# The front of an adaLN / S4 convolution / SwiGLU kernel in a new order: logs and right-hand sides first, two steps' tables, then u

## The chip, the cores and the metric

The kernel runs on one core of a Trainium2 chip. Times are device microseconds of that core, median of several runs. The engines of the core are TensorE (PE in the profile, its weight loads PEld), VectorE (DVE), ScalarE (ACT), GpSimd (POOL) and the queues that issue transfers, above all that of SyncE (SP). Each engine takes its own instructions in order and waits on semaphores for the others.

## The reference

For an input of 2048 rows and 640 columns, the reference computes

```
mod = silu(c) @ w_mod                      # six vectors of 640: sa, ca, ga, sb, cb, gb
h   = layernorm(x) * (1 + ca) + sa
K   = Re( sum_n C * exp(dt*A*l) * dt*B )   # one filter of 2048 taps per column, 128 states each
x   = x + ga * ( causal_conv(h, K) + h * Dskip )     # in the reference by FFT of length 4096
h   = layernorm(x) * (1 + cb) + sb
x   = x + gb * ( (silu(h @ w1) * (h @ w3)) @ w2 )    # inner width 1728
```

All of it is float32. The parameters A, B, C are complex numbers of 640 x 128.

## The kernel before, in words

The kernel has a first part, the convolution with everything that prepares it, and a second part, the feed-forward with its weights split in two for fast float32 matmuls. The change lies in the first some 160 us of the first part, called the front here; what follows is untouched.

**The filter.** A tap number is split as l = 64 a + b. For 16 channels (one step; there are 40) the kernel makes tables of the magnitudes and the phases of 128 states at 64 + 32 points, and a product on TensorE over the 128 states gives all taps of a channel. A step's work is a fixed series, each with a short name in the code: PH makes integer phases on POOL (two products, `phases`, L473 and L474); AB, CO and SI turn them into cosines and sines on ACT; PA, XA, PQ, XQ make exponents by matmuls against small right-hand sides r2, r1 and `sel` and an Exp on ACT (`exps` does a pair of steps); E1, E2, A1, A2 multiply magnitude by cosine and sine on DVE (L498, L501, L505, L509); `kg` is the product on TensorE; K, pt and uk scale it and make its first transform stage.

**The parameters.** `polar` (L239) turns A, B, C and dt into log magnitudes (`la`, `lm`, transposed on TensorE for the exponents) and integer phases (`thi`, `phi`). It is a generator in parts: the factors up to their squares; logarithm and angle; then the rows for `la` and `lm` and the last steps of the phase. It is done for the first 128 channels ahead of everything, and for the other 512 in the first four turns of the loop below. Its working space is the third of the `uk` buffers (`flat[2]`), the same room that later takes pieces of w_mod.

**The modulation.** `mod_sums` (L300) sums a piece of silu(c) @ w_mod: five matmuls, one for each block of 128 rows of K, the first four in the four groups of 32 columns of the array, the fifth again in the first group. A second matmul against the column `one4` adds the four groups. Eight such pieces (`mod_early`) give sa, ca and ga in the front, in the PSUM banks pb and pk in turn; five larger ones (`mod_cols`) come at the end of the front and give the feed-forward's vectors. `mod_shift` (L319) makes the row sa / (1 + ca), broadcasts it into PSUM by ten recorded matmuls (`pr`), copies it (`rrow`), and by a multiply (`rc`), twelve recorded matmuls (`ps`) and a copy makes `shift`, the row scaled by the transform of a constant.

**u.** `ln1_norm` normalizes two tiles of x, `u_stage1` (L395) makes the first transform stage of one tile in PSUM banks Z and A or B, adds the shift on the way out and stores u to DRAM. There are 16 tiles; `u_load` brings u back by frequency.

**Order.** A scheduler places each engine's instructions by their place in the program and by modelled readiness; ACT's instructions (`act`, `acopy`, `act_set`) keep the order of the program in all of the front. After the opening lines, a loop of ten turns (`tk`, L777) does the steps' tables, two u tiles a turn, the second pass of the parameters, and at its end the five `mod_cols`. Their w_mod pieces go through two rooms of `flat[2]`. When the last is done the pool `pre` closes, and the space goes to the convolution's second stage (`stage2`, L571). From there to 365 us rounds of four steps repeat one written order of words.

The opening, whose order is the subject, is this (L730 to 771, shortened):

```
first = polar(d0, V); next(first); next(first)
for j in range(4): ln1_load(j)
... r2; rest of first; do("PH", 0); r1
... five mod_early, loads
mod_shift(); act_set("natural_log_exp_and_others")
exps(0); ln1_norm(0); exps(2); ln1_norm(1)
do("PH", 1); do("PH", 2); AB, CO, SI of step 0
u_stage1(0); u_stage1(1); ln1_norm(2); AB, CO, SI of step 1
... three mod_early; mod_gate(); u_stage1(2); u_stage1(3)
```

## Time and profile before

| | us |
|---|---|
| median of three runs | 971.03 |
| the three runs | 970.67, 971.03, 975.4 |
| the profiled execution | 975.08 |
| its span, first to last instruction | 973.3 |
| PE busy in the span | 896.1 (92%) |
| DVE busy | 714.1 (73%) |
| ACT busy | 543.0 (56%) |
| POOL busy | 282.4 (29%) |

Rows of the profile give the engine, the line of the code (L102 is line 102), the operation, output and inputs with their shapes, how often it occurs, and its times. A row in the order of time begins with its start and its length in us; what stands in brackets is the idle time of the engine before it and what ended that. A line with x10 is several instructions of one kind merged, with the time from the first start to the last end. A row of the chain has only start, length and the instruction or the transfer. A row of a group has the busy time of all and the mean in ns. A float32 matmul of the code is recorded as two instructions. The clock is TensorE's granted clock as a share of full speed.

### The profile page before, as it was taken

Reading aid. Unit: us, or ns where it says so; the run is one execution under the profiler, and the core shown is the slowest. Engines: PE = TensorE matmul, PEld = TensorE weight load, DVE = VectorE, ACT = ScalarE, POOL = GpSimd, SP = SyncE. Lnnn points to the kernel's source line nnn. Section 1 sums busy time; section 2 is a strip of 40 time slices with the busy share of each in tenths; the row PEclk is TensorE's granted clock in tenths of the full one; section 3 lists DMA queues with packets and bytes.
Section 4 is the critical chain, followed back from the end, with each engine's and each line's share of the span. In section 5 each row is a group of like instructions: output and inputs, shape, how many; then the busy total and the mean of one; then the engine's idle time right before and its main releaser. Section 6 shows DMA issues by size and latency. Waiting matters only on the chain.

```text
span 973.3 us, 20145 instructions
## 1 busy us (share of the span) xinstructions
PE 896.1 (92%) x7984; PEld 675.4 (69%) x7984; DVE 714.1 (73%) x1259; ACT 543.0 (56%) x795; POOL 282.4 (29%) x278
## 2 busy tenths in 40 slices
PE   4978787889888899899999999999999999999998
PEld 2534444666666666567888888777888888888886
DVE  5598865999999996767666665677786766654675
ACT  4568675999999984236433333455743333333332
POOL 1372343455455641113422220121252222200000
PEclk8555777999999999899999999999999999999999
DMA  9463576655665688785213112895422221113443
GB/s 267 143 228 131 198 202 179 163 147 140 170 162 145 171 224 245 220 216 194 91 55 108 55 55 78 234 272 187 146 84 64 77 66 53 54 41 94 149 150 122
DMA packets 103571, 140.73 MB, mean 145 GB/s; under 512 B 20564, under 2 KB 62676, under 8 KB 103476
## 3 DMA queue, kind: packets, MB, share of 16 engines
q1 hardware_dynamic: 99668, 129.34, 46.0%
q0 software_dynamic: 2304, 7.74, 2.4%
q10 hardware_dynamic: 1504, 2.36, 0.8%
q8 instruction: 63, 1.03, 0.4%
q14 instruction: 32, 0.26, 0.1%
HBM read 107.94 MB, written 31.46 MB: 143 GB/s over the span
## 4 chain that ended last, share of the span: by engine, by line
PE 76%; ACT 9%; DVE 7%; DMA 4%; issue 3%; POOL 0%; ACTq 0%; SPq 0%; DVEq 0%; POOLq 0%
PE ps L102 55%; PE p L571 6%; ACT A L135 3%; PE pz L613 3%; PE pk L522 2%; PE pt L540 2%; ACT cs L135 2%; DMA zs<-zt 2%; PE pq L445 2%; PE pa L435 1%; PE pm L305 1%; PE pu L412 1%; ACT uk L138 1%; DMA uk<-in_w_mod_dram 1%; PE pm L316 1%
## 5 line engine op out<-in xcount | busy, mean ns | idle before, releaser
L102 DVE TENSOR_TENSOR s<-ps,s 128x512 f32<-128x512 f32 x138 | 94.9, 688 | 80.4 <-PE ps L102 79.5
L473 POOL TENSOR_TENSOR ph<-thi,iota 128x1024 int32<-128x1024 int32 x40 | 91.9, 2298 | 154.4 <-DVE A L505 54.0
L102 DVE TENSOR_TENSOR gl<-rw,gh 128x640 fp32r<-128x640 f32 x87 | 78.2, 899 | 65.2 <-ACT gh L102 65.1
L102 ACT CAST gh<-rw 128x640 fp32r<-128x640 f32 x87 | 63.3, 727 | 104.2 <-PE ps L102 63.4
L571 PE MATMUL p<-uk,s 128*64 128x256 f32 x640 | 79.4, 390 | 14.0 <-ACT uk L138 5.8
L102 PE MATMUL ps<-xA,gh 128*128 128x512 f32 x280 | 87.8, 392 | 0.4 <-ACT xA L102 0.4
L102 PE MATMUL ps<-gh,uh 128*128 128x512 f32 x224 | 87.5, 391 | 0.0
L102 PE MATMUL ps<-gl,uh 128*128 128x512 f32 x224 | 87.2, 389 | 0.0
L102 POOL TENSOR_TENSOR S<-rw 128x256 f32<-128x256 f32 x46 | 36.8, 801 | 170.7 <-DVE S0l L102 160.0
L102 PE MATMUL ps<-gh,ul 128*128 128x512 f32 x208 | 81.1, 390 | 0.0
L571 PEld LDWEIGHTS p<-uk,s 128*64 128x64 f32 x640 | 45.9, 139 | 37.8 <-issue 9.7
L498 DVE TENSOR_TENSOR E<-A,cs 128x1024 f32<-128x1024 f32 x40 | 60.4, 1511 | 3.2 <-ACT cs L135 2.5
L102 PEld LDWEIGHTS ps<-xA,gh 128*128 128x128 f32 x280 | 52.1, 188 | 13.0 <-ACT xA L102 0.9
L102 PE MATMUL ps<-xA,gl 128*128 128x512 f32 x140 | 54.6, 390 | 0.0
L474 POOL TENSOR_TENSOR ph<-ph,phi 128x512 int32<-128x512 int32 x40 | 48.5, 1213 | 5.0 <-DVE phi L297 2.0
L540 PE MATMUL pt<-s,K 128*64 128x128 f32 x640 | 48.3, 291 | 1.4 <-ACT uk L138 1.4
L505 DVE TENSOR_TENSOR A<-A,ph 128x1024 f32<-128x1024 f32 x40 | 48.9, 1223 | 0.0
L102 ACT ACTIVATE s<-ps 128x512 f32<-128x512 f32 (+1 forms) x33 | 19.7, 597 | 51.3 <-PE ps L102 51.3
L102 PEld LDWEIGHTS ps<-gl,uh 128*128 128x128 f32 x224 | 42.0, 188 | 9.0
L102 PEld LDWEIGHTS ps<-gh,uh 128*128 128x128 f32 x224 | 42.0, 188 | 8.7
L522 PE MATMUL pk<-E 128*32 128x64 f32 x1280 | 45.9, 233 | 1.5 <-issue 0.9
L613 PE MATMUL pz<-Y,i 64*128 64x128 f32 x640 | 44.4, 282 | 2.8 <-issue 2.7
(255 smaller groups left out, 2270.4 us busy)
## 6 DMA issues: line engine op xcount, KB each, us to landing
rw<-in_w_dram SPq DMA_DIRECT2D x52, 320.0 KB
us<-u SPq DMA_DIRECT2D x16, 640.0 KB
s<-in_s_dram SPq DMA_DIRECT2D x40, 256.0 KB
i<-in_i_dram SPq DMA_DIRECT2D x40, 256.0 KB
rw<-in_wg_dram SPq DMA_DIRECT2D x31, 320.0 KB
rw<-in_wu_dram SPq DMA_DIRECT2D x28, 320.0 KB
uk<-us SPq DMA_DIRECT2D x32, 256.0 KB
zs<-zt SPq DMA_DIRECT2D x32, 256.0 KB
```

The source lines that it names most:

```text
L102: ins = fn(*args, **kw)
L135: return tc.keep_in_program_order(S.activation(*args, **kw))
L138: return tc.keep_in_program_order(S.copy(out, in_))
L445: keep(PE.matmul(pQ[s][:, rr, :256], w[r, t, :], bc(sel[r, js], 2, NA) if i else r1[r, js, :], start=(i == 0), stop=(i == 1), tile_positio ...
L473: hold(G.tensor_tensor(p, bc(thi[:, sl], 2, NPH), bc(iota, 1, SD), op=OP.mult))
L474: keep(G.tensor_tensor(p[:, :, :NA], p[:, :, :NA], bc(phi[:, sl], 2, NA), op=OP.add))
L498: keep(V.tensor_tensor(EC[s][:, :, 1:3, :], AA[s][:, :, 1:3, :], mid(cs[s]), op=OP.mult))
L505: keep(V.tensor_tensor(A[:, :, 1:3, :], A[:, :, 1:3, :], mid(ph[s]), op=OP.mult))
L522: keep(PE.matmul(pk[dq * 32:dq * 32 + 32, g, :], x[:, g * 4 + dq, 1, :], x[:, g * 4 + dq, 0:3:2, :], start=(st == 0), stop=(st == 1), tile ...
L540: keep(PE.matmul(pt[c * 64:c * 64 + 64, g, :], kk[:, g, :], s1[:, c, :], start=True, stop=True, tile_position=(0, c * 64)))
L571: keep(PE.matmul(p2[par * 64:par * 64 + 64, pi, c, :], s2[:, pi * 2 + par, c * 64:c * 64 + 64], uk[:, 0:kn + 1:kn, f, :], start=True, stop ...
L613: ins = keep(PE.matmul(pz[:, par, (g % 2) * 2 + pi, :], i1[r, pi, c, :], Y[r, pi, c, :], start=(c == 0), stop=(c == 1), tile_position=(par ...
```

## The change

The constants `selx` and `stepx` get a small array of their own, `selstep`, which is the first transfer on SP's queue; `misc` has a new column c1c instead. r2, made from them, is the first DVE instruction after the initial memsets. `polar` becomes a class with the same instructions in parts that can be ordered: for the first 128 channels the order is now factors, log, rows, angle, phase, and the rows of `la` and `lm` have a split space each. The second pass keeps its places in the loop. In the sums the fifth block is divided into four quarters of the columns, one for each group. The broadcast of the row takes 128 columns of weights in place of 64, and `shift` is read from it by two scaled copies on ACT; `rc` and `ps` are gone. In the opening, PH, AB, CO and SI of steps 0 and 1 and the first pair of exponents come before the modulation sums; the tables of step 0 follow LN1's first two tiles; the product of step 0 and the tables of step 1 follow the first two u tiles. Of the three late sums, the second is in bank Z in place of pk.

```diff
-    misc = np.concatenate([selx, stepx, s1r, c1, one4, toq, tog], axis=1)
+    misc = np.concatenate([s1r, c1, np.tile(c1[0], 2)[:, None], one4, toq, tog], axis=1)
+    selstep = np.concatenate([selx, stepx], axis=1)
...
+    l2f = [t3[:, DC + 2 * DC * i:DC + 2 * DC * (i + 1)] for i in range(2)]
...
+    nc.sync.dma_start(selstep, a["selstep"])
     nc.sync.dma_start(cT, a["c"])
...
-    def polar(cs, E):
...
+    class Polar:
...
+        def rows(self):
...
             for i, dst in enumerate((la, lm)):
...
-            both = l2[:, :2 * nk * P].rearrange("n (b s c) -> n b s c", s=2, c=32)
+                both = self.l2[i].rearrange("n (b s c) -> n b s c", s=2, c=32)
...
     def mod_sums(w, pm):
 
         n = w.shape[2]
-        for k in range(KD):
-            g = slice(k % 4 * NA, k % 4 * NA + NA)
-            PE.matmul(pm[g, :n], scb[:, k], w[:, k, :], start=(k < 4), stop=(k > 0), tile_position=(0, g.start))
+        last = [slice(g * n // 4, (g + 1) * n // 4) for g in range(4)]
+        for g in range(4):
+            r = slice(g * NA, g * NA + NA)
+            PE.matmul(pm[r, :n], scb[:, g], w[:, g, :], start=True, stop=False, tile_position=(0, r.start))
+        for g, c in enumerate(last):
+            r = slice(g * NA, g * NA + NA)
+            PE.matmul(pm[r, c], scb[:, 4], w[:, 4, c], start=False, stop=True, tile_position=(0, r.start))
...
         for k in range(KD):
-            PE.matmul(pr[:64, k * P:(k + 1) * P], r[:, k:k + 1].broadcast_to([P, 64]), ident, start=True, stop=True)
+            PE.matmul(pr[:, k * P:(k + 1) * P], r[:, k:k + 1].broadcast_to([P, P]), ident, start=True, stop=True)
+        for hh in range(2):
+            h = slice(hh * 64, hh * 64 + 64)
+            act(shift[h], pr[h, hh * 320:hh * 320 + 320], AF.Copy, scale=c1c[h])
         V.tensor_copy(rrow[:64], pr[:64, :D])
-        rc = pm_.tile([P, WC], F32, name="part", bufs=2)[:, :KD * 2 * NA].rearrange("p (k c) -> p k c", k=KD)
-        V.tensor_tensor(rc, bc(c1, 1, KD), bc(r, 2, 2 * NA), op=OP.mult)
...
-        V.tensor_copy(shift, ps[:, :320])
...
+    V.tensor_tensor(r2, bc(selx, 2, NB), bc(stepx[:, :NB], 1, NA), op=OP.mult)
     act_set("natural_log_exp_and_others")
...
-    first = polar(d0, V)
-    next(first)
-    next(first)
+    first = Polar(d0, V, l2f)
+    first.factors()
+    first.log()
+    first.rows()
+    first.angle()
+    first.phase()
+    V.tensor_tensor(r1, bc(selx, 2, NA), bc(stepx[:, NB:], 1, NA), op=OP.mult)
     for j in range(4):
         ln1_load(j)
-    V.tensor_tensor(r2, bc(selx, 2, NB), bc(stepx[:, :NB], 1, NA), op=OP.mult)
-    for _ in first:
-        pass
     do("PH", 0)
-    V.tensor_tensor(r1, bc(selx, 2, NA), bc(stepx[:, NB:], 1, NA), op=OP.mult)
+    do("PH", 1)
+    for n in ("AB", "CO", "SI"):
+        do(n, 0)
+    for n in ("AB", "CO", "SI"):
+        do(n, 1)
+    act_set("natural_log_exp_and_others")
+    exps(0)
     for i, t in enumerate(("pb", "pk", "pb", "pk", "pb")):
         mod_early(i, wm[i], t)
...
     mod_shift()
-    act_set("natural_log_exp_and_others")
-    exps(0)
     ln1_norm(0)
+    for n in ("E1", "E2", "A1", "A2"):
+        do(n, 0)
     exps(2)
-    ln1_norm(1)
-    do("PH", 1)
-    do("PH", 2)
-    for n in ("AB", "CO", "SI"):
-        do(n, 0)
     u_stage1(0)
     u_stage1(1)
+    ln1_norm(1)
+    do("kg", 0)
+    for n in ("E1", "E2", "A1", "A2"):
+        do(n, 1)
+    do("PH", 2)
     ln1_norm(2)
-    for n in ("AB", "CO", "SI"):
-        do(n, 1)
-    for i, t in enumerate(("pb", "pk", "pb")):
+    for i, t in enumerate(("pb", "Z", "pb")):
         mod_early(5 + i, wg[i], t)
     mod_gate()
     u_stage1(2)
     u_stage1(3)
-    rest = polar(d1, G)
+    rest = Polar(d1, G, [l2, l2])
...
             if tk == 2:
-                next(rest)
+                rest.log()
+                rest.angle()
...
         if tk == 0:
-            next(rest)
+            rest.factors()
         if tk == 3:
-            next(rest, None)
+            rest.rows()
+            rest.phase()
```

127 lines of the change are left out of this document (64 added, 63 removed).

## The prediction

> **What bounds the kernel now.** I read the page first, then the stretches, then the chain of waits, then the order of time in the front. The profiled execution took 975.08 us, 1.78 us more than its span. It is the upper of the three runs (970.67, 971.03, 975.4), 4.05 us above their median; differences found in the trace are therefore taken off its own 975.08 and then off the median 971.03.
>
> ```profile
> span 973.3 us, 20145 instructions
> ...
> PEclk8555777999999999899999999999999999999999
> ```
>
> The clock line says that TensorE is granted about half speed from the second slice (24 us) to the fourth and about 0.7 to the seventh. Next, the stretches (length, then busy us of PE, PEld, DVE, ACT, POOL, then the granted clock, DMA share and GB/s):
>
> ```profile
> 0.00:10.00 10.00, 0.48 (x8) 0.31 (x9) 4.62 (x19) 3.24 (x7) 0.20 (x4) 1.00 0.86 227
> 10.00:20.00 10.00, 6.56 (x33) 3.18 (x25) 8.37 (x24) 4.75 (x10) 2.98 (x2) 0.80 1.09 341
> 20.00:30.00 10.00, 10.00 (x53) 5.74 (x52) 2.71 (x10) 2.71 (x4) 0.00 (x0) 0.50 0.97 290
> 30.00:40.00 10.00, 7.57 (x38) 5.56 (x36) 6.59 (x20) 4.74 (x6) 5.19 (x7) 0.50 0.39 142
> 40.00:50.00 10.00, 9.28 (x76) 3.90 (x74) 5.95 (x11) 7.12 (x8) 5.54 (x5) 0.66 0.07 30
> 50.00:110.00 60.00, 51.82 (x564) 28.22 (x564) 54.29 (x102) 42.94 (x53) 26.44 (x29) 0.54 0.48 177
> 110.00:164.00 54.00, 39.75 (x574) 21.85 (x576) 39.32 (x64) 34.98 (x40) 21.52 (x14) 0.83 0.74 209
> ```
>
> DVE is full from 50 to 110 us (54.29 of 60) but idle for 21.76 of the first 50 us. PE at half clock is nearly full beside it (51.82 of 60). The front therefore has two engines at their limit after 50 us and much idle DVE before. Where the front ends, the chain shows:
>
> ```profile
> 139.26 9.70 DMA uk<-in_w_mod_dram
> ...
> 149.09 2.69 PE pm L305 x10
> ...
> 163.52 3.23 PE p L571 x16
> ```
>
> The first product of the convolution's second stage (L571) starts at 163.5 us, behind the last five column sums and the w_mod transfers that feed them. These transfers are issued only when the second parameter pass has left its room, which the next two rows show: the phase is written at 110.34 and the queue issues at 110.84.
>
> ```profile
> 110.34 0.42 DVE L297 TENSOR_SCALAR phi<-uk 128x512 int32<-128x512 f32 x1
> ...
> 110.84 2.31 SPq L206 DMA_DIRECT2D uk<-in_w_mod_dram  x3
> ```
>
> So whatever brings the 110.3 us point forward brings the front's end forward, as long as the 53 us behind it keep their length. The rounds that follow repeat one written order, with no dependence on when they began; I carry a gain of the front unchanged to the end.
>
> **The change, part by part.** First the parameter pass of the first channels.
>
> ```profile
> 8.43 2.29 DVE L737 TENSOR_TENSOR r<-misc 128x2048 fp32r<-128x2048 f32 x1
> ...
> 10.63 0.29 DVE L257 SCALAR_TENSOR_TENSOR uk<-uk 128x128 f32<-128x128 f32 x1
> ...
> 13.75 1.94 POOL L473 TENSOR_TENSOR ph<-thi,iota 128x1024 int32<-128x1024 int32 x1 [13.30 <-DVE thi L274]
> 13.85 1.99 DVE L288 TENSOR_TENSOR uk<-lt,uk 128x128 f32<-128x128 f32 x1
> ...
> 16.51 0.37 ACT L138 CAST la<-pT 128x256 fp32r<-128x256 f32 x1 [2.84 <-PE pT L291]
> ...
> 17.12 0.29 DVE L288 TENSOR_TENSOR uk<-lt,uk 128x128 f32<-128x128 f32 x1
> ...
> 18.39 0.37 ACT L138 CAST lm<-pT 128x256 fp32r<-128x256 f32 x1 [1.30 <-PE pT L291]
> ```
>
> The table r2 (2.29 us) goes ahead of everything. Its operand selstep is 64 KB and one more issue on SP's queue ahead of c and the parameters; by the row at 110.84 an issue lasts at most 2.31 / 3 = 0.77 us, so the parameters land up to 0.8 us later; I take half of that. r2 then fills DVE time that is idle while the parameters travel, and L257, which now waits until 10.63 behind r2, no longer does; I take half a microsecond gained there. Rows before angle means that la and lm wait for no arctangent: five DVE steps and a table load go out of their way, so lm, now 18.39, comes at about 13.5. The two halves l2f remove the wait of the second cast on the first transposes; that is inside this. Angle and phase then come later in that pass, covered by the transposes and the first exponents' matmuls.
>
> At one place a price must be weighed. L288 took 1.99 us beside POOL's product and 0.29 without it, so one meeting costs 1.7 us. The new order brings a second phase product into this pass. I take one meeting as now, and 1.7 us more as the upper end. The Trainium skill, page "SBUF — State Buffer", section "Who interferes with whom", states that a DVE instruction with two SBUF inputs and a GpSimd instruction that reads SBUF lock each other out for a whole instruction; the trace agrees (1.99 against 0.29 us). By that rule both products would block, and the sum would come 1.7 us higher.
>
> Second, the sums and the shift of LN1.
>
> ```profile
> 31.51 0.16 DVE L317 COPY cols<-pm 128x2 f32<-128x2 f32 x1 [1.19 <-PE pm L316]
> ...
> 34.62 2.40 PE L330 MATMUL pr<-ident,cols 128*64 128x128 f32 x10 [2.43 <-DVE cols L326]
> ...
> 36.81 1.76 PE L339 MATMUL ps<-ident,part 128*64 128x128 f32 x12
> ...
> 39.08 0.47 DVE L341 COPY shift<-ps 128x320 f32<-128x320 f32 x1
> ...
> 43.59 3.46 PE L305 MATMUL pm<-uk,scb 128*32 128x256 f32 x20
> ...
> 158.55 1.91 PE L305 MATMUL pm<-uk,scb 128*32 128x384 f32 x10 [1.99 <-DMA uk<-in_w_mod_dram]
> ```
>
> At half clock two sums of 256 columns take 3.46 us, 1.73 each. The code's five matmuls are ten in the row, two passes each; by their tile positions four K blocks can run side by side and the fifth follows alone, so a pass is 1.73 / 4 = 0.43; the fifth in quarters takes a quarter of it, 0.11. A sum becomes 1.73 - 2 x 0.32 = 1.08, 0.65 less. Five such sums, then two of 256 and one of 128 columns: 7.5 x 0.65 = 4.9 us of PE. It could also be nothing, if three more weight loads per pass (8 in place of 5) are what sets the pace; they are hidden behind matmuls in the row. The removed matmuls ps give 1.76 us of PE, their copy 0.47 of DVE, and the multiply for rc on the same 128x320 shape I price at the same 0.47. The broadcast keeps ten matmuls of 128 columns (2.40), with wider weights. Two scaled copies of 64x320 go to ACT instead; ACT's 128x256 cast above is 0.37, so 0.8 to 1.0 us there, before LN1's first tiles.
>
> Third, the order. With no exponents' matmuls among them, the five sums' chain should end some 6 us before 31.5. Two table steps move from behind the first u tiles to before them.
>
> ```profile
> L498 DVE TENSOR_TENSOR E<-A,cs 128x1024 f32<-128x1024 f32 x12 | 16.3, 1359 | 1.4 <-ACT cs L135 0.7 <-PE pk L522 0.7
> ...
> L505 DVE TENSOR_TENSOR A<-A,ph 128x1024 f32<-128x1024 f32 x11 | 13.6, 1237 | 0.0
> ...
> L501 DVE TENSOR_TENSOR E<-A,cs 128x512 f32<-128x512 f32 x11 | 10.3, 935 | 0.0
> L509 DVE SCALAR_TENSOR_TENSOR A<-ph,A 128x512 f32<-128x512 f32 x11 | 8.0, 727 | 0.0
> ```
>
> A step's tables take 1.36 + 1.24 + 0.94 + 0.73 = 4.26 us, two of them 8.5 us, taken out of the full stretch and put where DVE is idle. On ACT, the sines of two steps and their one table load come before the first exponents:
>
> ```profile
> 20.07 1.02 ACT L135 ACTIVATE A<-pa 128x1024 f32<-128x1024 f32 x1
> ...
> 30.15 0.60 ACT L135 ACTIVATE A<-pq 128x512 f32<-128x512 f32 x1 [2.92 <-PE pq L445]
> ...
> 43.43 1.04 ACT L135 ACTIVATE cs<-ph 128x1024 f32<-128x1024 int32 x1
> 44.49 1.28 ACT L135 ACT_TABLE_LOAD   x1
> 45.79 1.15 ACT L135 ACTIVATE cs<-cs,hp 128x1024 f32<-128x1024 f32 x1
> ...
> 47.79 0.67 ACT L138 COPY u<-pu 128x640 f32<-128x640 f32 x1
> ```
>
> A step's sines take 1.04 + 1.15 + 1.04 (the sine as the absolute value) = 3.23 us, a pair of exponent steps 2 x (1.02 + 0.60) = 3.24, a load 1.28. With the first phases at about 17.5, ACT does 6.5 of sines, 1.3 of load and 3.2 of exponents and ends them at 28.5, now 30.75. Shift, LN1 of two tiles and the second exponents follow; the first u copy, now 47.79, comes at about 36. Behind these waiting ACT steps are queued the shift and LN1, and PE's u matmuls wait for both.
>
> The moved steps pass other queues too. POOL makes the second step's phases ahead of LN1's small steps: its 2.98 and 0.00 us busy from 10 to 30 leave room, no cost. SP's loads keep their order behind selstep; the u stores come earlier, into the stretch with a DMA share of 0.07. The first kernel product keeps its PSUM bank until the gate, so one late sum takes bank Z between two u tiles: sum, copy and columns, about 2.5 us in which the next u tile's first half waits; PE has the other late sums and the product itself meanwhile, so I count nothing, and 2.5 us if that cover is gone.
>
> The sum goes by DVE. Up to 110 us it is busy 4.62 + 8.37 + 2.71 + 6.59 + 5.95 + 54.29 = 82.53 us, less 0.94 for rc and the shift's copy: 81.6. Its idle time up to there is now 27.5. In the new order I estimate 3.5 before the parameters (5.4 less r2, plus the issue), 2 in the rest of the pass, 4 while ACT does sines and exponents (copies of the sums, r1 and the statistics of LN1 remain to fill it; 20 to 40 us had 10.7 idle), 2 up to 50 us (now 4.05), and 6 in the loop (now 5.7): 17.5. The phase would be written at 81.6 + 17.5 = 99.1, or 11.2 us before 110.34.
>
> PE as the check: it is busy 85.7 us up to 110, and 85.7 - 4.9 - 1.8 = 79.0 from 9.5 on could end at 88.5 with no idle at all; 99.1 leaves 10.6 idle where it has about 15 now. That is tight at half clock, so I take 2 us off: 9.2. In the 53 us behind, the last sum (1.91 on the chain) loses three eighths, 0.7; the one before it is followed by a transfer and counts nothing. In all 9.9, say 10 us. From 975.08 that is 965.1; from the median, 961.0.
>
> **The rivals.** First, TensorE is the bound. At half clock PE and DVE wait for each other, and what moves on DVE leaves PE's own work where it is. If the front follows PE with today's idle time, only the five early sums' 5 x 0.65 = 3.3 us remain of the gain: 968. For it: 51.82 of 60 busy. Against it: the same PE line has idle time in 30 to 40 us that the tables now fill. That the moved work changes nothing at the end because transfers set 163.5 anyway falls in with this; against that stands the issue at 110.84, half a microsecond behind the phase.
>
> Second, slower. PE takes its queue in order. If the first steps' pq matmuls stand ahead of the modulation sums, they wait for ACT, whose sines now precede the exponents, and the sums wait behind them. Four sums and their columns (1.1 + 1.0 each) would begin when the first exponents are out, at about 27 to 30, and end near 38 in place of 31.7; shift and LN1's first u follow 6 us later than now. It decides once the first u copy on ACT comes after 47.79; with the 6 us carried through the u tiles, the time is 977.
>
> Third, TensorE goes to full clock in the denser front.
>
> ```profile
> 62.81 1.34 PE L404 MATMUL pu<-rrow,misc 1*64 1x320 f32 x8 [1.52 <-DVE u L417]
> ...
> 108.48 0.77 PE L404 MATMUL pu<-rrow,misc 1*64 1x320 f32 x8
> ```
>
> The same eight matmuls took 1.34 us at half and 0.77 at full clock. PE's 51.82 would then be near 30 and DVE alone the bound; its 5.7 us of idle time in that stretch would go too: 956. Against it: PE was busy 10.00 of 10.00 in 20 to 30 us and the clock stayed 0.50. The Trainium skill, "TensorE: Matmul & The Clock Gate", Part 1, says about 3.4 us of sustained activity releases the clock; the trace does not agree in that stretch.
>
> **How the numbers follow.** A measurement here tells about 0.5%, 4.9 us, from no change (the three runs span 4.7). Forecast 0.56, full clock 0.11, TensorE bound 0.16, slower 0.17. The likeliest gives 961, in its own range 955 to 967 (the port's 1.7, bank Z's 2.5 and sums that save less on one side, DVE idle shrinking to 12 on the other). Below 966.2 lie nearly all of forecast and full clock and a little of the TensorE case: 0.70. Within: 0.16. Above 975.9: half of the slower case and what else I do not see, 0.14. The range for 8 in 10 reaches from 951 to 974.
>
> **What the new profile would show.** The first exponents on ACT end before 30 us; cols of the fifth sum before 28; L288 twice at about 0.3, or once at 2; a sum at half clock about 1.1 us; the first u copy on ACT near 36; DVE busy over 8 of 10 from 30 us on; phi of the second pass near 100 and the first L571 near 153. The forecast is wrong if DVE still idles 20 us before 50, if the u tiles begin later than now, or if the stretch between the phase and L571 grows by what the front saved.

## The result, and the profile after

The changed kernel takes 981.63 us (median of seven runs, 979.13 to 984.93), the kernel before in the same session 972.07 (seven runs, 970.67 to 975.4). The ratio is 1.0092, 95% interval 1.0068 to 1.0116. The change makes the kernel slower by 0.9%; 961.0 was forecast.

The profiled execution of the changed kernel took 979.54 us (span 977.8), near the lowest of its runs; the one shown before took 975.08, near the highest of its own. The two traces therefore differ by 4.5 us where the medians differ by 9.6: they show half of the loss. The span and clock lines of the page of the changed kernel:

```profile
span 977.8 us, 20279 instructions
...
PEclk9555587999999999999999999999999999999999
```

The same stretches as in the prediction, of the changed kernel (start and end, length, busy us of PE, PEld, DVE, ACT, POOL, then clock, DMA share, GB/s):

```profile
0.00:10.00 10.00, 0.00 (x0) 0.00 (x0) 6.18 (x22) 3.13 (x7) 0.20 (x4) 1.00 0.77 215
10.00:20.00 10.00, 9.28 (x56) 4.81 (x56) 4.31 (x17) 3.53 (x9) 1.90 (x1) 1.00 1.11 340
20.00:30.00 10.00, 5.66 (x57) 4.33 (x57) 5.71 (x25) 6.22 (x7) 4.86 (x5) 0.67 0.82 230
30.00:40.00 10.00, 7.79 (x51) 4.29 (x50) 8.84 (x12) 8.96 (x11) 4.21 (x4) 0.50 0.58 214
40.00:50.00 10.00, 9.22 (x116) 4.76 (x114) 8.25 (x15) 3.52 (x5) 2.06 (x3) 0.50 0.34 117
50.00:110.00 60.00, 50.99 (x494) 24.55 (x488) 47.16 (x94) 39.50 (x49) 26.59 (x30) 0.53 0.43 152
110.00:164.00 54.00, 41.51 (x624) 25.56 (x624) 41.36 (x61) 36.19 (x42) 21.06 (x14) 0.78 0.77 217
```

DVE is busy 33.29 us of the first 50, where it was 28.24: the tables did move there. But from 50 to 110 us it is busy only 47.16 of the 60, where it was 54.29. The idle time was moved behind the tables, not removed. Up to 110 us DVE is busy 80.45 us (81.6 was forecast) and idle 29.55 (17.5 was forecast, 27.5 it was).

The order of time in the opening (start, length, instruction; in brackets the idle time before it and what ended that):

```profile
12.39 0.37 ACT L139 CAST la<-pT 128x256 fp32r<-128x256 f32 x1 [1.50 <-PE pT L307]
...
15.04 0.37 ACT L139 CAST lm<-pT 128x256 fp32r<-128x256 f32 x1 [2.08 <-PE pT L307]
...
19.00 0.42 DVE L330 COPY part<-pm 128x256 f32<-128x256 f32 x1 [2.00 <-PE pm L328]
...
22.25 0.23 DVE L316 TENSOR_SCALAR phi<-uk 128x128 int32<-128x128 f32 x1
...
22.62 1.04 POOL L490 TENSOR_TENSOR ph<-ph,phi 128x512 int32<-128x512 int32 x1 [3.64 <-DVE phi L316]
...
23.70 1.06 ACT L136 ACTIVATE cs<-ph 128x1024 f32<-128x1024 int32 x1 [6.17 <-POOL ph L490]
...
26.63 0.16 DVE L340 COPY cols<-pm 128x2 f32<-128x2 f32 x1 [0.70 <-PE pm L339]
...
31.27 1.94 ACT L136 ACTIVATE A<-pa 128x1024 f32<-128x1024 f32 x2
...
34.59 1.05 ACT L136 ACTIVATE shift<-pr,misc 64x320 f32<-64x320 f32 x2
35.66 1.73 ACT L136 ACTIVATE x<-x,rs 128x640 f32<-128x640 f32 x2
37.42 1.94 ACT L136 ACTIVATE A<-pa 128x1024 f32<-128x1024 f32 x2
...
44.62 0.69 ACT L139 COPY u<-pu 128x640 f32<-128x640 f32 x1 [0.69 <-PE pu L428]
...
63.06 0.69 ACT L139 COPY u<-pu 128x640 f32<-128x640 f32 x1 [10.57 <-issue]
```

Two rows of the kernel before, for comparison:

```profile
17.33 0.22 DVE L297 TENSOR_SCALAR phi<-uk 128x128 int32<-128x128 f32 x1
...
57.30 0.69 ACT L138 COPY u<-pu 128x640 f32<-128x640 f32 x1 [1.83 <-PE pu L412]
```

ACT copies every second u tile, so its first two copies of u are those of the first and the third tile; they are called the first and the third u copy here. The log rows come earlier (la 12.39 for 16.51, lm 15.04 for 18.39), the sums end earlier (26.63 for 31.51), the first u copy comes earlier (44.62 for 47.79). Between them lies a hole: the phase of the first channels comes at 22.25, where it came at 17.33, because its last four steps stand in DVE's queue behind copies of the sums and of their columns that wait for PE (idle 2.00 before the first of them, 1.04 before the second). POOL's phases wait for it (3.64), and ACT, whose first sine now stands ahead of everything else, waits 6.17 us for POOL. The first exponents come at 31.27 instead of 20.07. The third u copy comes at 63.06; it was at 57.30. From there on every copy of u on ACT is some 4 to 7 us later than before, to the end of the second parameter pass:

```profile
105.70 0.42 DVE L316 TENSOR_SCALAR phi<-uk 128x512 int32<-128x512 f32 x1
...
118.64 1.25 SPq L209 DMA_DIRECT2D uk<-in_w_mod_dram  x2
...
119.07 1.01 ACT L139 CAST lm<-pT 128x1024 fp32r<-128x1024 f32 x1 [3.18 <-PE pT L307]
```

The last rows of the front in the chain of waits:

```profile
152.26 10.38 DMA uk<-in_w_mod_dram
...
167.33 3.26 PE p L587 x16
```

The phase of the second pass, at 105.70, is 4.6 us earlier than before, but la (114.36) and lm of that pass are 6.2 and 7.5 us later (108.17 and 111.61 before). The row of lm in the kernel before:

```profile
111.61 1.01 ACT L138 CAST lm<-pT 128x1024 fp32r<-128x1024 f32 x1 [1.91 <-PE pT L291]
```

The next view lists what SP's queue waited for from 100 to 130 us (total, times, longest); first the changed kernel, then the one before:

```profile
SPq L209 <- DVE uk L304: 5.3, 1, 5.3
...
SPq L209 <- PE pT L307: 2.4, 1, 2.4
SPq L209 <- DVE phi L316: 1.2, 1, 1.2
```

```profile
SPq L206 <- DVE phi L297: 5.9, 1, 5.9
```

Before, the w_mod load (L206, now L209) waited for the phase alone, and its three issues went out from 110.84 on. Now one goes out behind the phase, at 106.2, and the other two wait for lm's rows (L304) and its transposes, until 118.64. The first product of the second stage (L571, now L587) starts at 167.33 instead of 163.52. The kernel ends 812.2 us behind it, before 811.6.

### The profile page after: what moved, and what is told of

Same layout as the page of the kernel before. It is cut to its first block, busy times and chain, and to the rows that moved or that the text cites. A ratio compares the mean times of both kernels' runs of the same rounds, so it can differ in the third digit from the quotient of the medians.

```text
span 977.8 us, 20279 instructions
## 1 busy us (share of the span) xinstructions
PE 895.3 (92%) x8050; PEld 675.2 (69%) x8050; DVE 715.4 (73%) x1257; ACT 543.6 (56%) x797; POOL 278.1 (28%) x278
## 4 chain that ended last, share of the span: by engine, by line
PE 77%; ACT 9%; DMA 5%; DVE 4%; issue 3%; POOL 2%; ACTq 0%; SPq 0%; DVEq 0%; POOLq 0%
PE ps L103 55%; PE p L587 6%; PE pz L629 3%; PE pt L556 3%; PE pk L538 2%; ACT A L136 2%; DMA zs<-zt 2%; ACT cs L136 2%; DMA uk<-in_w_mod_dram 2%; PE pa L451 1%; PE pu L428 1%; PE pq L461 1%; PE pu L420 1%; PE pm L325 1%; ACT uk L139 1%
## 5 line engine op out<-in xcount | busy, mean ns | idle before, releaser
L587 PE MATMUL p<-uk,s 128*64 128x256 f32 x640 | 79.8, 390 | 16.1 <-issue 7.2
L587 PEld LDWEIGHTS p<-uk,s 128*64 128x64 f32 x640 | 46.1, 138 | 40.1 <-issue 12.3
L490 POOL TENSOR_TENSOR ph<-ph,phi 128x512 int32<-128x512 int32 x40 | 50.8, 1269 | 6.4 <-DVE phi L316 3.6
L556 PE MATMUL pt<-s,K 128*64 128x128 f32 x640 | 50.5, 295 | 0.6 <-ACT uk L139 0.6
```

What stands on the lines that cost most here:

```text
L490: keep(G.tensor_tensor(p[:, :, :NA], p[:, :, :NA], bc(phi[:, sl], 2, NA), op=OP.add))
L556: keep(PE.matmul(pt[c * 64:c * 64 + 64, g, :], kk[:, g, :], s1[:, c, :], start=True, stop=True, tile_position=(0, c * 64)))
L587: keep(PE.matmul(p2[par * 64:par * 64 + 64, pi, c, :], s2[:, pi * 2 + par, c * 64:c * 64 + 64], uk[:, 0:kn + 1:kn, f, :], start=True, stop ...
```

## The experiments

Ratios are those to the kernel before, run on the same chip in the same session, with 95% intervals. First each part alone, then the late u tiles, then the tables, then what was left.

**The parts one by one.** The first kernel is the one before with the new sums and the new shift (`mod_sums`, `mod_shift`) and its old order; the second is the changed kernel with both put back, so that the new order and the new parameter pass stand alone.

Their edits are the change's own hunks of these two functions, e1 taking them over and e2 taking them back; e1 also has the column c1c, at the end of the old `misc`:

```diff
-    misc = np.concatenate([selx, stepx, s1r, c1, one4, toq, tog], axis=1)
+    misc = np.concatenate([selx, stepx, s1r, c1, one4, toq, tog, np.tile(c1[0], 2)[:, None]], axis=1)
```

> The kernel before with the two changes of arithmetic alone: sums over four column groups and LN1's shift from the broadcast; the order is the old one. Theory A (the new order lets TensorE's queue take the late sums and the gate in the middle of the third u tile, so that ACT idles 10.57 us there and the front's early gain is spent): these parts are not at fault, 968 to 973 us, against 972 for before. Theory B (the arithmetic costs: eight weight loads a sum in place of five, wider broadcast weights, two copies on ACT): 976 or more. A sum of 256 columns at half clock should take about 1.1 us instead of 1.7 in either case.

> The new order alone: the changed kernel with the old sums and the old shift. Theory A: the loss is in the order, 979 to 986 us, and the copy of the third u tile on ACT still comes after 60 us. Theory B: 973 or less, since the arithmetic would be the cost. Theory C (POOL's products run one behind the other from 48.8 to 64.8 us and hold up LN1's small steps and DVE): as A, 979 to 986.

e1 took 986.75 us, ratio 1.0178 (1.0154 to 1.0202); e2 975.88, ratio 1.0056 (1.0031 to 1.0081). Sums and shift are the worse half when they stand in the old order. ACT's rows of e1 in the order of time show why:

```profile
34.41 1.06 ACT L135 ACTIVATE shift<-pr,misc 64x320 f32<-64x320 f32 x2 [15.77 <-PE pr L335]
...
36.78 1.94 ACT L135 ACTIVATE A<-pa 128x1024 f32<-128x1024 f32 x2
```

ACT keeps the order of the program. Two scaled copies, 1.06 us together, wait 15.77 us for the whole modulation chain, and the first exponents, at 20.07 before, stand behind them. This says nothing of the shift itself, so sums and shift were tried again, apart from one another. e8 is the kernel before with the new `mod_sums`, e7 the changed kernel with the old one. e14 is the kernel before with the new `mod_shift`, behind the first exponents:

```diff
-    mod_shift()
     act_set("natural_log_exp_and_others")
     exps(0)
+    mod_shift()
```

> The kernel before with the four-group sums alone. The run with sums and shift together lost 17 us, and in it ACT stood behind the two shift copies (first exponents at 36.8 us in place of 20.1). Theory: the shift on ACT ahead of the exponents was that loss; the sums alone give 966 to 971, and the first exponents come at 20 us again. Rival: the sums themselves disturb the old order: 975 or more.

> The changed kernel with the old sums (fifth block whole in the first group) and everything else as changed. The new order alone lost about 6 us, with both new parts of arithmetic about 9 to 10. Theory B' (the four-group sums cost something here, by eight weight loads and by the later order they lead to): 974 to 977, as the order alone. Theory C (the cause is POOL's and TensorE's queue order, to which the sums' length is nothing): 979 to 984.

> The kernel before with the new shift alone, and its two scaled copies placed on ACT behind the first two steps' exponents instead of ahead of them. Theory D (a copy on ACT delays what stands behind it in ACT's fixed order, here LN1's first tiles): pr still near 34.6, the shift copies at about 37, LN1's first tiles from 34.0 to about 39, the first u copy 1 to 3 us later than 47.79; 972 to 975 us. Rival (the cost of the new shift was only the exponents that stood behind it): PE and DVE are spared 1.76 and 0.94 us, 968 to 970 us.

e8: 972.87 us, 1.0023 (0.9999 to 1.0048). e7: 981.14, 1.0099 (1.0061 to 1.0137), against 1.0092 with the new sums. The sums make no difference that these intervals show, in either order.

e7 shows something else. With the old sums the same steps come earlier: the phase of the first channels at 19.18, the first sine at 20.62 after a wait of 3.30 us, LN1's first tiles at 33.39 (34.00 in the kernel before), the first u copy at 41.07. The third u copy still comes at 61.96. The second pass of e7, on DVE and ACT:

```profile
100.53 0.42 DVE L316 TENSOR_SCALAR phi<-uk 128x512 int32<-128x512 f32 x1
...
114.32 1.01 ACT L139 CAST lm<-pT 128x1024 fp32r<-128x1024 f32 x1 [3.38 <-PE pT L307]
```

The phase is 9.8 us earlier than before, nearly the 11.2 that were forecast, and yet the first product of the second stage starts at 163.06 in the chain, half a microsecond earlier than before. (The profiled execution of e7 took 975.33, near the lowest of its six runs.)

The sums are as short as forecast all the same; one of 256 columns and one of 128 in a row at half clock, PE's rows of a kernel below (e12):

```profile
51.84 1.08 PE L325 MATMUL pm<-uk,scb 128*32 128x256 f32 x8 [1.61 <-DVE u L440]
...
52.91 0.65 PE L325 MATMUL pm<-uk,scb 128*32 128x128 f32 x8
```

From the start of the first to the start of the next are 1.07 us, before 1.73. e14: 973.42, 1.0037 (1.0013 to 1.0061): with the exponents out of its way the new shift still costs some 4 us, by the interval 1 to 6. Its copies came at 33.61 and LN1's first tiles directly behind them at 34.69, not at 39 as was expected, and the first u copy at 47.19; the third was at 59.72. Some 0.7 us of delay of LN1's first tiles (34.00 before) do not explain 4; by which wait the shift costs them is open.

**The late third u tile.** In the changed kernel PE does the three late sums, their columns and the gate's product between the second and the third u tile. Three kernels moved what stands there: e3 puts sums and gate behind the fourth tile, e4 puts step 2's sines on ACT ahead of them, e9 holds POOL's phases from step 3 on and the second pass's products behind LN1's small steps of the same turn.

```diff
+    u_stage1(2)
+    u_stage1(3)
     for i, t in enumerate(("pb", "Z", "pb")):
         mod_early(5 + i, wg[i], t)
     mod_gate()
-    u_stage1(2)
-    u_stage1(3)
```

```diff
+    for n in ("AB", "CO", "SI"):
+        do(n, 2)
     for i, t in enumerate(("pb", "Z", "pb")):
```

```diff
-        do("PH", tk + 3)
+        if tk >= 5:
+            do("PH", tk + 3)
...
                 ln1_norm(tk + 3)
+                with tc.issue_after(root[0].ins):
+                    do("PH", tk + 3)
...
+            with tc.issue_after(root[0].ins):
                 rest.factors()
```

> The changed kernel with the three late sums and the gate moved behind the third and fourth u tiles. Theory A: the copy of the third u tile on ACT comes at 51 to 54 us in place of 63.06, ACT's idle time before it falls from 10.57 to under 4 us, and the time falls by 6 to 10, to 971 to 976. Theory C: POOL still runs without a gap from 49 to 65 and the fourth LN1 pair still waits for it, so the time stays at 979 or more even if the copy comes earlier.

> The changed kernel with the cosines and sines of the third step put ahead of the late sums, so that ACT has 3.2 us of work and a table load of 1.3 us where it idled 10.57. Theory A: ACT's later queue is 4.5 us shorter after the third u tile, but PE's order there is unchanged: 975 to 979. Theory C: the sines wait for POOL's third phases, which come at 52.9, and ACT's order then holds the u copy back too: 979 to 984.

> The changed kernel with POOL's phases of steps 3 and later, and the second parameter pass's products, issued only behind LN1's small steps of the same turn. Theory C (POOL's early phases lock DVE and hold LN1's fourth pair from 62.0 to 64.7 us, and DVE's gate steps L361 and L363 are stretched by 1.9 us): the gate's matmul comes by 59 in place of 60.8, the third u tile's copy by 61 and the time is 973 to 977. Theory A' (TensorE's queue alternates the late sums' columns with the u tiles, whatever POOL does): the copy stays near 63 and the time at 979 or more.

All three are slower than the changed kernel: e3 987.6, ratio 1.0203 (1.0171 to 1.0235); e4 984.65, 1.0164 (1.0142 to 1.0186); e9 988.67, 1.0203 (1.0165 to 1.0241). In e3 the third copy comes at 53.62, as that theory wanted, and the next pays for it. DVE's and ACT's rows of e3:

```profile
67.31 0.16 DVE L403 SCALAR_TENSOR_TENSOR rs<-mv,rs 128x2 f32<-128x2 f32 x1 [6.63 <-POOL rs L402]
...
75.49 0.69 ACT L139 COPY u<-pu 128x640 f32<-128x640 f32 x1 [16.83 <-PE pu L428]
```

A 0.16 us step of LN1 waits 6.63 us for POOL, which has phases and factors ahead of it in its queue; the copies of the late sums stand behind that step on DVE, PE waits for them, and ACT waits 16.83 us for the u tile. e9 takes exactly that wait away and brings the third copy to 59.57, and the loss comes back later: its lm is at 120.91, its first product of the second stage at 173.12. In e4 the third copy did not move (63.05). None of the three places holds a loss that can be undone there alone. That the late sums or POOL's order have no part in it is not shown, since each edit disturbs other queues too.

**The tables.** e11 is the changed kernel with the tables of steps 0 and 1 and the first product back in the loop; e12 is e11 with the old `mod_shift`.

```diff
     ln1_norm(0)
-    for n in ("E1", "E2", "A1", "A2"):
-        do(n, 0)
     exps(2)
...
     ln1_norm(1)
-    do("kg", 0)
-    for n in ("E1", "E2", "A1", "A2"):
-        do(n, 1)
```

> The changed kernel with the tables of steps 0 and 1 and the product of step 0 left to the loop as before. If moving them forward was worth the 8.5 us of DVE time that I counted, the time is 985 or more. If the tables forward free the phase buffers and so start POOL too early (theory C), POOL's phases of step 5 come after 70 us again and the time is 972 to 977.

> The changed kernel with the tables of steps 0 and 1 and the first product back in the loop, and with the old shift (rc, ps and a copy on DVE). The order, the new parameter pass and the new sums stay. Theory D (the tables moved forward and the shift put on ACT each cost some 5 us of their own, by 981.6 against 976.5 and 981.1 against 975.9): about 971 to 972 us, the first LN1 tiles on ACT without two shift copies before them, the third u tile's copy near 58. Rival (both costs are one wait, seen twice): 975 to 977 us, as with the tables alone put back.

e11: 976.53, ratio 1.0059 (1.0032 to 1.0086). e12: 975.29, 1.0063 (1.0039 to 1.0086). The tables that were to gain 8.5 us seem to cost some 3 (1.0092 against 1.0059; the intervals overlap), and only beside the new shift: e2, with the tables forward and the old shift, stands at 1.0056, no worse than e12, which has neither (its sums are the new ones, and e7 and e8 show no difference from these). The theory that tables and shift each cost 5 us of their own falls: with the tables back, the shift makes no difference. Some 6 us of loss remain with neither.

**What remained.** e13 is the kernel before with the new parameter pass alone (`selstep`, r2 first, the class `Polar`), e19 is e13 with the new `mod_sums`; the opening behind the pass is the old one in both.

```diff
-    first = polar(d0, V)
-    next(first)
-    next(first)
+    first = Polar(d0, V, l2f)
+    first.factors()
+    first.log()
+    first.rows()
+    first.angle()
+    first.phase()
     for j in range(4):
         ln1_load(j)
```

> The kernel before with the new parameter pass alone: selstep first on the queue, r2 first on DVE, factors, log, rows, angle, phase, split space for the rows. The opening behind it, the sums and the shift are the old ones. Theory D: la near 12.4 and lm near 14 to 15 instead of 16.5 and 18.4, first exponents on ACT at 17 to 18 instead of 20.07, phases some us later with no one waiting for them before 43 us; 967 to 969 us. Rival (the first exponents are not what the front waits for, the modulation sums are): 970 to 971 us, the fifth cols copy still at 31.5.

> The kernel before with the new parameter pass and the new sums, the opening and the shift old. All theories: fifth cols copy near 27, first exponents near 20, 967 to 970 us, not slower than the kernel before. If sums and pass together free the front's first half, the first u copy comes near 44 and the time is below 967 us; if the two cancel each other, as each alone showed no difference, 969 to 971 us.

e13: 969.12, 0.9998 (0.9973 to 1.0024). e19: 971.63, 1.0013 (0.9985 to 1.0040). Level with before, both. So what remains in e12 lies in the order behind the pass. Three kernels each undo one part of that order in e12: e16 the bank of the second late sum, e17 the place of LN1, e18 the place of phases, sines and first exponents. e15 moves in the full change the first exponents alone.

```diff
-    for i, t in enumerate(("pb", "Z", "pb")):
+    for i, t in enumerate(("pb", "pk", "pb")):
```

```diff
+    ln1_norm(1)
     u_stage1(0)
     u_stage1(1)
-    ln1_norm(1)
```

```diff
     do("PH", 0)
-    do("PH", 1)
-    for n in ("AB", "CO", "SI"):
-        do(n, 0)
-    for n in ("AB", "CO", "SI"):
-        do(n, 1)
-    act_set("natural_log_exp_and_others")
-    exps(0)
...
     mod_shift()
+    act_set("natural_log_exp_and_others")
+    exps(0)
     ln1_norm(0)
     exps(2)
+    do("PH", 1)
+    for n in ("AB", "CO", "SI"):
+        do(n, 0)
...
     ln1_norm(2)
+    for n in ("AB", "CO", "SI"):
+        do(n, 1)
```

```diff
+    act_set("natural_log_exp_and_others")
+    exps(0)
     do("PH", 0)
...
-    act_set("natural_log_exp_and_others")
-    exps(0)
     for i, t in enumerate(("pb", "pk", "pb", "pk", "pb")):
```

> The kernel with the new order but tables in the loop and the old shift, and the second late sum in bank pk again, so that no sum stands between two u tiles in bank Z. Theory Z (the u tiles wait for the late sums through bank Z): third u copy from 63.64 to 57 to 59, time 970 to 972 us. Rival (the bank does nothing; PE's order is the same without it): third u copy above 62, 974 to 976 us.

> The same kernel with LN1 of tiles 2 and 3 ahead of the first two u tiles again; bank Z and the sines stay. Theory L (the third tile's LN1 comes late: its ACT steps at 50.70, POOL's small steps for it wait behind nothing but start only at 47.81): LN1 of the second pair near 42 to 44, third u copy near 58, 970 to 972 us. Rival: tiles wait for PE all the same, third u copy above 62, 974 to 976 us.

> The same kernel with phases of step 1, sines of steps 0 and 1 and the first exponents where the kernel before has them; bank Z and the later LN1 stay. Theory S (PE spends its full clock of the first 30 us waiting for ACT's sines, and the exponents' products then meet the sums at half clock): first exponents near 20, fifth cols copy near 27 to 28, first u copy near 46, 970 to 972 us. Rival (sines and exponents are where ACT was idle anyway): 974 to 976 us.

> The changed kernel with the first pair of exponents ahead of the sines of steps 0 and 1 on ACT (two table loads of 1.28 us more). Theory D (the exponents' products wait in PE's banks A and B for ACT, which waits for POOL's first phases): first exponents on ACT near 16 to 18 instead of 31.27, the fifth cols copy a few us later than 26.63, the second pair of exponents and with them the tables earlier; 976 to 979 us. Rival (the late exponents harm nothing, since the tables of step 0 wait for the sines anyway): 981 to 984 us, the two loads standing in LN1's way.

e16: 974.51, ratio 1.0063 (1.0037 to 1.0090), just that of e12: the bank costs nothing. Its third u copy is at 55.41, in a profile that was the slowest of its twelve runs, so an early third copy is no sure sign of a gain. e17: 981.05, 1.0128 (1.0092 to 1.0164): LN1's new place is the better one in the new order. e18: 971.41, 1.0025 (0.9999 to 1.0051): of the three only the sines seem to count, though this interval and that of e12 still overlap. e15: 979.72, 1.0102 (1.0068 to 1.0137): the first exponents by themselves, with the sines still ahead of LN1 and the second exponents, recover nothing. In e15 they end at 28.68, as forecast for the change, but the fifth sum's columns come at 30.86 and LN1's first tiles at 37.67.

The last two turn this round. e20 adds to e19 the one move that e18 took back (r1 on DVE and the first phases on POOL also change places in the program); e21 takes that move out of the full change.

```diff
     do("PH", 0)
+    do("PH", 1)
+    for n in ("AB", "CO", "SI"):
+        do(n, 0)
+    for n in ("AB", "CO", "SI"):
+        do(n, 1)
+    act_set("natural_log_exp_and_others")
+    exps(0)
     for i, t in enumerate(("pb", "pk", "pb", "pk", "pb")):
...
     mod_shift()
-    act_set("natural_log_exp_and_others")
-    exps(0)
     ln1_norm(0)
     exps(2)
     ln1_norm(1)
-    do("PH", 1)
     do("PH", 2)
-    for n in ("AB", "CO", "SI"):
-        do(n, 0)
...
     ln1_norm(2)
-    for n in ("AB", "CO", "SI"):
-        do(n, 1)
```

```diff
     do("PH", 0)
-    do("PH", 1)
-    for n in ("AB", "CO", "SI"):
-        do(n, 0)
-    for n in ("AB", "CO", "SI"):
-        do(n, 1)
     act_set("natural_log_exp_and_others")
     exps(0)
...
     ln1_norm(0)
+    exps(2)
+    do("PH", 1)
+    for n in ("AB", "CO", "SI"):
+        do(n, 0)
     for n in ("E1", "E2", "A1", "A2"):
         do(n, 0)
-    exps(2)
     u_stage1(0)
     u_stage1(1)
     ln1_norm(1)
+    for n in ("AB", "CO", "SI"):
+        do(n, 1)
     do("kg", 0)
```

> The kernel with the new pass and the new sums (level with before, 1.0013), and with one more move alone: the phases of step 1, the sines of steps 0 and 1 and the first exponents ahead of the sums. Shift, LN1's places, bank pk and the tables are the old ones. Theory S (six sines, and the wait for POOL's phases ahead of them, stand in ACT's fixed order before LN1's first tiles and the second exponents): ACT idle some 6 us before 24, second exponents from 33.3 to 39 or 41, third u copy from 54.1 to 58 or later, 975 to 977 us. Rival (the loss needs the other moves as well): 970 to 973 us.

> The changed kernel with the phases of step 1 and the sines of steps 0 and 1 behind the second exponents, and the first exponents at once after the first phases; the forward tables, the first product, the shift on ACT, bank Z and LN1's places stay. Theory S: first exponents near 20, LN1's first tiles near 35 still (behind the shift), second exponents 36 to 38 instead of 37.4, sines then, the tables later; 975 to 978 us. Rival (in the full change the tables and the shift alone hold the front back, whatever the sines do): 980 to 982 us.

e20: 976.95, ratio 1.0084 (1.0055 to 1.0113), where e19 stood at 1.0013 (0.9985 to 1.0040). The move alone makes a loss of 0.7%. ACT's and PE's rows of e19, in the order of time:

```profile
19.78 1.94 ACT L136 ACTIVATE A<-pa 128x1024 f32<-128x1024 f32 x2
...
31.64 1.73 ACT L136 ACTIVATE x<-x,rs 128x640 f32<-128x640 f32 x2 [4.26 <-DVE rs L410]
...
35.80 1.08 ACT L136 ACTIVATE A<-pq 128x512 f32<-128x512 f32 x2 [0.61 <-PE pq L468]
...
44.25 0.67 ACT L139 COPY u<-pu 128x640 f32<-128x640 f32 x1
...
106.58 1.01 ACT L139 CAST lm<-pT 128x1024 fp32r<-128x1024 f32 x1 [1.91 <-PE pT L307]
...
157.57 3.46 PE L594 MATMUL p<-uk,s 128*64 128x256 f32 x16
```

and of e20, with the step of LN1 on DVE that its first tiles wait for:

```profile
24.60 1.06 ACT L136 ACTIVATE cs<-ph 128x1024 f32<-128x1024 int32 x1 [7.03 <-POOL ph L497]
...
31.61 0.16 DVE L410 SCALAR_TENSOR_TENSOR rs<-mv,rs 128x2 f32<-128x2 f32 x1 [0.68 <-POOL rs L409]
...
32.16 1.94 ACT L136 ACTIVATE A<-pa 128x1024 f32<-128x1024 f32 x2
...
37.39 1.72 ACT L136 ACTIVATE x<-x,rs 128x640 f32<-128x640 f32 x2
...
45.13 0.60 ACT L136 ACTIVATE A<-pq 128x512 f32<-128x512 f32 x1 [3.71 <-PE pq L468]
...
47.25 0.68 ACT L139 COPY u<-pu 128x640 f32<-128x640 f32 x1
...
115.15 1.01 ACT L139 CAST lm<-pT 128x1024 fp32r<-128x1024 f32 x1 [3.99 <-PE pT L307]
...
164.66 3.23 PE L594 MATMUL p<-uk,s 128*64 128x256 f32 x16
```

In e19 ACT does the first exponents at 19.78 while the phases are being made, and waits for LN1 (rs at 31.44), which it then does at once. In e20 it waits 7.03 us for the phases, does six sines and a table load, and only then the exponents; LN1's first tiles, whose rs is ready at 31.77, start at 37.39, 5.75 us later than in e19. The second exponents end at 45.73, in e19 at 36.88, and meet the late sums on PE there. The u tiles start 3.0 us later (44.25 to 47.25), lm of the second pass is 8.6 us later, the first product of the second stage 7.1, the profiled time 6.2 (970.41 to 976.56).

Part of this difference may be the clock's. Up to 50 us it was alike in both (1.00 from 10 to 40 us, then 0.73 and 0.72), so the later opening is not. But from 70 to 80 us it was 0.84 in e19 and 0.50 in e20, and the u copies, 3 to 4 us apart up to 69.50 and 73.43, are 6.0 apart at the next (89.97 and 96.00). e18, at 0.50 from 50 to 100 us, has this copy at 92.46, so the clock does not explain all. The 0.7% rests on the medians of twelve and nine runs, not on these two traces.

e21, in which the move is taken out of the full change, is no better but much worse: 987.58, 1.0188 (1.0159 to 1.0217). In its trace the exponents stand first, the fifth sum's columns come at 30.56 (26.63 in the full change), and ACT waits 9.80 us for the broadcast before it can copy the shift at 38.52. LN1's first tiles come at 39.60, not near 35 as expected. The forward tables then wait for sines that end at 50.5; they run on DVE from 50.03 to 55.29, and the next u halves (L433, L434) stand behind them until 55.21. The third copy is at 73.23. With the tables forward, taking back the sines makes things worse: this change could not be repaired by that move alone.

No version beat the kernel before. What stays open: how the 9 us of the full change divide between the sines, the tables and the shift, and by which wait. The sines alone make 0.7% on e19; without the tables (e11, e12) or without the new shift (e2) no more than that shows; but the parts are not additive, and an interval of half a per cent does not separate them further.

## Why the prediction was wrong

Three steps failed: the point whose gain was carried to the front's end, the time at which ACT's first sine gets its phases, and DVE's idle time in the sum.

**What bounds.** The front's end does carry through to the kernel's end: 811.6 us lie between the first product of the second stage and the end before, 812.2 after, 812.8 in e19 and 811.9 in e20. What failed is the signpost within the front. "Whatever brings the 110.3 us point forward brings the front's end forward, as long as the 53 us behind it keep their length": the phase did come forward, to 105.70, and the stretch behind it grew from 53 to 61.6. The phase was the last to release the room before, as the issue at 110.84 said, but lm's rows and transposes release it too; the transposes ran from 110.48 to 111.57, hidden under the 2.31 us of the queue's own issues. In the changed kernel they come last, by 13 us, and set the issue of 118.64. One of several releases had been taken for the only one. e7 shows it most plainly: its phase is 9.8 us early and its front ends half a microsecond early. In all twenty kernels, before and after among them, the first product starts 46 to 52 us behind the start of lm's cast, but 52 to 66 us behind the phase.

**The parameter pass.** la gained 4.1 us; lm came at 15.04 (13.5 was forecast). "Angle and phase then come later in that pass, covered by the transposes and the first exponents' matmuls" was wrong too: they are covered by nothing, for the new order makes the first phase the head of ACT's queue. The port was rightly counted at one meeting at most: the two casts' subtractions (L304 now) took 0.28 and 0.29.

**"With the first phases at about 17.5, ACT does 6.5 of sines, 1.3 of load and 3.2 of exponents and ends them at 28.5"** is the step of the opening that failed. The lengths were right (23.70 to 29.96 for six sines, 1.28, 3.4); the start was not. The first phases are whole on POOL at 23.66, six microseconds later, since the phase's last four steps were scheduled between the sums' copies on DVE, and these wait for PE. The sum had counted what DVE does there and not in which order. e20 against e19 shows what the move costs: the wait of 7.03 us and the six sines ahead of LN1 and the second exponents make 0.7%. How much of it is the late start is not shown, for no run has the phases at 17.5. In e7 ACT's first sine comes 3 us earlier (20.62 for 23.70) and the first u copy 3.5 us earlier, and the loss is the same, 1.0099: in the full change these 3 us were worth nothing that shows.

**"Two table steps ... 8.5 us, taken out of the full stretch and put where DVE is idle."** They were put there, and the busy time came out as forecast (80.45 for 81.6). The ledger's other side was wrong: 11.5 us of idle time to 50 us were allowed, 16.71 came; 6 in the loop were allowed, 12.84 came. Without these tables in the loop DVE had longer waits: from 50 to 110 us it waited 5.1 us for POOL's steps of LN1 (1.7 before), 3.2 for ACT once and some 4 for PE. "Tight at half clock" was priced at 2 us; PE was busy 50.99 of those 60 us, DVE 47.16 and ACT 39.50, so no engine was full, and which chain of waits held the stretch stays open. e2 and e11 show what the moved tables were worth: nothing with the old shift, and with the new one a loss of some 3 us in place of a gain.

**Sums and shift.** The price of a sum was right (1.07 for 1.08), and the end of the five sums too (26.63, about 25.5 was meant). The 4.9 us of PE were worth nothing that the intervals of e8 and e7 show, alone or together with the rest. ACT's copies of the shift took the 0.8 to 1.0 us forecast (1.05 for both), but e14 shows 0.37% for the shift alone and e1 1.8% where other work stands behind it in ACT's order. Bank Z was rightly counted at nothing (e16).

**The rivals.** Slower was given 0.17, with the time 977, and the direction is what came. Its mechanism was half right: ACT's sines ahead of the exponents, and shift and LN1 behind them. That pq matmuls would hold back the sums did not happen in the changed kernel (fifth sum at 26.63); in e15 and e21, with the exponents first, it came at 30.86 and 30.56. And "it decides once the first u copy on ACT comes after 47.79" named the wrong mark: that copy came at 44.62 and the kernel was slower. The third copy was a better mark but not a sure one either (e16). TensorE as the bound would have had a gain left; there was none. Full clock did not come: 0.53 from 50 to 110 us.

## What to carry to other kernels

An engine that keeps the program's order is one queue: before a step is moved to its head, ask when its input is ready in the new order, not in the trace of the old, and what is ready earlier and now stands behind it. Idle time on the fullest engine is only a gain where that engine's inputs come sooner too; a ledger of busy time per engine says how much work there is, not that the gaps can be filled. And where several instructions release a buffer, the one that was last before need not be last after: list them all.

## What the runs showed of the hardware

The half clock of TensorE is not bound to a place in the program. In the profile of before it is granted 0.50 from 20 to 40 us; in e19 and e20 1.00 from 10 to 40 us, then 0.73 and 0.72 to 50 and 0.65 and 0.53 from 50 to 110. The changed kernel and e12, whose orders are the same up to the shift, had 0.67 and 1.00 from 20 to 30 us. In e16 the front ran at a higher clock (1.00 up to 50 us, 0.83 from 50 to 110) and low slices came later too. Clock line of e16's page:

```profile
PEclk9997587999999989889999999999999999999999
```

Its first product of the second stage is at 161.51, 5.8 us before that of the changed kernel, and its time is 981.12 all the same: 819.6 us lie behind that product, where it is 809 to 817 in all the others. Whether the low slices account for that is not shown. The kernel before went from 964.5 to 976.2 us within one session. Two profiles can therefore differ by more than the change does; only the medians tell the versions here apart.

VectorE and GpSimd meet outside the parameter pass too. LN1's step on DVE of 128x2 values took 0.16 us alone (29.93) and 1.85 beside a phase product (32.29) in the changed kernel, as it did in the kernel before (1.85 at 36.57):

```profile
29.93 0.16 DVE L403 SCALAR_TENSOR_TENSOR rs<-mv,rs 128x2 f32<-128x2 f32 x1 [0.68 <-POOL rs L402]
...
32.29 1.85 DVE L403 SCALAR_TENSOR_TENSOR rs<-mv,rs 128x2 f32<-128x2 f32 x1 [1.09 <-POOL rs L402]
```

This is what the Trainium skill, "SBUF — State Buffer", section "Who interferes with whom", states of a DVE instruction with two SBUF inputs; the trace agrees. DVE's step ended with GpSimd's product (32.22 to 34.13); it lost 1.69 us, and the 128x128 step in the prediction's rows lost 1.70, whatever their own size.
